# Longformer attention into a softplus layer: batch 2 at three slots a pair, other orders of loading, a second queue, and products that nobody reads

## The chip, the cores and the metric

The kernel runs on one core of a Trainium2 chip. The core has five engines that run side by side: TensorE (matrix products, into the accumulator memory PSUM), VectorE, ScalarE (activation functions such as Exp and Ln), GpSimd (POOL in the profile) and SyncE (SP), which here only issues DMA transfers. Each engine works through its own instructions in order, and semaphores hold an instruction until what it needs is there. The metric is the device time of one execution in microseconds (us), the median of several. TensorE's clock can be granted in full or at a lower share; the profile shows which.

## The reference

Eight batches of attention with 8 heads, 576 positions and 64 numbers per head. A query sees the keys within 32 positions and 8 global keys; the 8 global positions see everything. The result, 4608 tokens of 512 numbers, goes through a layer of 2048 softplus units and back to 512.

```python
scores = scale * np.matmul(q, k.transpose(0, 1, 3, 2))
mask = np.abs(pos[:, None] - pos[None, :]) <= window
mask = mask | is_global[:, None] | is_global[None, :]
scores = np.where(mask, scores, -1000000000.0)
attn = np.exp(scores - np.max(scores, axis=-1, keepdims=True))
attn = attn / (np.sum(attn, axis=-1, keepdims=True) + 1e-09)
x = np.matmul(attn, v)          # then (batch, position) x (head, number): 4608 x 512
h = x @ w_in                    # 4608 x 2048
g = np.maximum(h, 0.0) + np.log1p(np.exp(-np.abs(h)))
return g @ w_out                # 4608 x 512
```

## The kernel before

**Dense layers.** The 4608 tokens are nine tiles of 512. The main loop runs over tiles n = 0 to 9 and, in each, over 16 steps; a step is called a slot here, numbered 16 n + s. `mm1(n, s)` (L395) makes 128 of the 2048 units for tile n: four products of 128x512 into one of two PSUM buffers, then Exp (L403) and Ln (L404) on ScalarE. `mm2(n - 1, s)` (L408) makes a quarter of one 128-token block of the output of the tile before: four products; every fourth one is copied by VectorE (L418) and stored by SP (L419). So tile 0 has slots with first-layer products alone, tiles 1 to 8 have both, and the last 16 slots have second-layer products alone. The first weight comes in four chunks of 512 units (`load_w_in`, slots 4c to 4c + 3 of a tile need chunk c), the second in four chunks of rows (`load_w_out`); both are issued by GpSimd and converted to bf16 on the way.

**Attention** goes by batch and by pair of heads, four pairs a batch. Keys and queries come in rows of six positions (`load_runs`, one DMA a pair), are cast to bf16 (`cast_runs`) and transposed on TensorE (`transposes`, L253), with copies out of PSUM on VectorE (on ScalarE for the queries of batch 0). The columns of the 8 global positions are appended to each tile of 120 positions: for batches 0 and 1 by products with a one-hot matrix (L263), for the later ones from `glob_T`, which comes from DRAM through `gather`, `load_global_columns` and `global_columns` and is copied by GpSimd. `scores` are two groups of products, each followed by Exp; `mask` multiplies by a mask on VectorE; `sums` and `values` are passes of 12 products over the masked exponentials, with a matrix of ones and with V. `inv_ln` and `inv_exp` make 1 / sum as exp(-ln) on ScalarE; `scale_x` (L353) multiplies on VectorE into `xT`, which the dense layers read. `glob_sums`, `glob_norm` and `glob_out` do the same for the 8 global queries; `glob_out` (L369) is eight small GpSimd copies at positions held in registers. V is cast by GpSimd (`cast_v`, L120) with its global rows in the last 8 partitions of each tile (`load_v_rows`); batch 0 instead adds a second pass with the global rows `VG`, which `value_globals` makes by products.

**Buffers.** Scores, sums and values share one ring of PSUM regions, three in batch 0 and two afterwards; transposes have a ring of their own. The float rows of keys, queries and V have one buffer each, so the rows of a batch can be loaded only after those of the one before have been cast. `junk`, a slice of the second weight's tile, holds ones, and `warm` multiplies it by itself into a buffer that nobody reads.

**Order.** Everything is written out in order by hand. The prologue (L504 to L568) does batch 0, starts loads and casts of batch 1, then V's gather on GpSimd (behind `glob_out`), the gathers of keys and queries on SP, and `warm(4)`. In the main loop a plan says what is done after `mm1` (half 0) and after `mm2` (half 1) of each slot:

```python
for s in range(16):
    if n < n_tiles:
        mm1(n, s)
    attend(16 * n + s, 0)
    if n:
        mm2(n - 1, s)
    attend(16 * n + s, 1)
```

`at(g, half, ...)` puts a step there. From batch 4 on a pair takes four slots: transposes at half-slots 0 and 1 of the pair, scores at 4, sums and values at 8, the normaliser at 9, scaling at 10. Batches 1 to 3 (`START`) take two slots a pair from slots 3, 20 and 30, with the same numbers halved. `LOAD` and `CAST` say at which slots rows are loaded and cast; DMAs of SP and stores stand in one queue, and casts, gathers, weight loads and `glob_out` in GpSimd's one.

## Time and profile before

| | |
|---|---|
| median of 6 runs | 387.02 us (386.18 to 388.53) |
| the profiled execution | 385.48 us, its span 383.9 us |
| TensorE busy | 345.0 us (90%) |
| ScalarE busy | 275.2 us (72%) |
| VectorE busy | 183.3 us (48%) |
| GpSimd busy | 119.4 us (31%) |
| mean granted TensorE clock | 0.959 |

| stage | from to (us of the span) |
|---|---|
| prologue | 0 to 38.03 |
| tile 0, slots 0 to 15 | 38.03 to 75.19 |
| tiles 1 and 2, slots 16 to 47 | 75.19 to 163.30 |
| tiles 3 to 5, slots 48 to 95 | 163.30 to 273.70 |
| tile 6 to the end | 273.70 to 383.9 |

All times come from one profiled execution, from its first to its last instruction. PE is TensorE, PEld its loading of weights, DVE VectorE, ACT ScalarE, POOL GpSimd, SP the DMA queue of SyncE; L400 is line 400 of the kernel. Rows of the timeline give start, length, engine, line, operation, output and inputs, how many instructions are merged in the row and, in brackets, how long the engine was idle before and what ended that.

### The profile page before, as it was taken

How to read it: one execution, taken by the hardware profiler on the slowest of the kernel's cores; microseconds unless marked ns; L12 is line 12 of the kernel's file. 1: busy time of each engine (PE TensorE's matmuls, PEld its weight loads, DVE VectorE, ACT ScalarE, POOL GpSimd, SP SyncE). 2: the span in 40 equal slices, each digit the busy share in tenths (PEclk: the TensorE clock that was granted, in tenths of full speed). 3: DMA queues.
4: the chain of work that ended last, by engine and by line, in shares of the span. 5: the costliest groups of instructions: out<-in, count | busy, mean ns of one | idle time of the engine just before them, and what ended most of it. 6: DMA issues, size and time to landing. Idle time of an engine off the chain costs nothing.

```text
span 383.9 us, 7411 instructions
## 1 busy us (share of the span) xinstructions
PE 345.0 (90%) x2761; PEld 176.4 (46%) x2801; DVE 183.3 (48%) x485; ACT 275.2 (72%) x438; POOL 119.4 (31%) x275
## 2 busy tenths in 40 slices
PE   6587877798997889999999999999999999999984
PEld 3464443344544444555455545554554444444432
DVE  7664277415766664766567556656554200100111
ACT  5742698757876886888888888887888767776500
POOL 7961770446419304434081309311100100000000
PEclk9556899989999999999999999999999999999999
DMA  7999549979938605580669156700000010010111
GB/s 172 247 258 212 98 73 210 247 152 252 154 96 210 130 30 150 152 161 38 155 166 155 57 148 163 130 28 29 29 27 30 27 56 27 27 56 27 55 56 55
DMA packets 62495, 43.64 MB, mean 114 GB/s; under 512 B 40932, under 2 KB 57444, under 8 KB 62460
## 3 DMA queue, kind: packets, MB, share of 16 engines
q1 hardware_dynamic: 57836, 38.86, 42.2%
q0 software_dynamic: 4480, 4.31, 6.8%
q8 instruction: 22, 0.36, 0.4%
q14 instruction: 13, 0.11, 0.1%
q10 hardware_dynamic: 144, 0.01, 0.0%
HBM read 37.92 MB, written 9.81 MB: 124 GB/s over the span
## 4 chain that ended last, share of the span: by engine, by line
PE 56%; issue 11%; DMA 11%; POOL 7%; SPq 6%; DVE 4%; ACT 1%; another core or an unknown queue 1%; POOLq 1%; DVEq 0%
PE o L414 25%; PE hp L400 22%; PE av L325 4%; PE sc L291 2%; DMA q_f<-in_q_dram 2%; PE tp L258 2%; SPq L105 2%; SPq L96 2%; DMA v_f<-v_global_rows 2%; DMA v_f<-in_v_dram 2%; POOL V L122 2%; POOL qb L118 2%; DVE ex L304 2%; DMA q_global_rows<-in_q_dram 2%; DMA q_rows<-q_global_rows 1%
## 5 line engine op out<-in xcount | busy, mean ns | idle before, releaser
L400 PE MATMUL hp<-xT,w_in_t 128*128 128x512 bf16 x548 | 147.6, 386 | 3.8 <-POOL xT L372 2.3
L414 PE MATMUL o<-w_out_t,gt 128*128 128x512 bf16 x565 | 145.4, 381 | 4.4 <-DVE ot L418 3.3
L403 ACT ACTIVATE e<-hp 128x512 f32<-128x512 f32 x144 | 86.0, 597 | 60.6 <-PE hp L400 57.6
L404 ACT ACTIVATE gt<-e 128x512 bf16<-128x512 f32 x144 | 90.7, 630 | 4.5
L414 PEld LDWEIGHTS <-gt 128*128 128x128 bf16 x576 | 54.1, 98 | 67.7 <-issue 8.7
L400 PEld LDWEIGHTS <-w_in_t 128*128 128x128 bf16 x576 | 53.1, 99 | 65.9 <-issue 9.8
L418 DVE COPY ot<-o 128x512 f32<-128x512 f32 x36 | 24.8, 690 | 84.9 <-PE o L414 79.6
L304 DVE TENSOR_TENSOR ex<-ex,mask 128x1008 bf16<-128x1008 bf16 (+1 forms) x56 | 44.6, 805 | 28.7 <-ACT ex L299 27.8
L372 POOL COPY xT<-xg 128x4 bf16 x64 | 12.9, 201 | 126.9 <-DVE xg L367 123.5
L299 ACT ACTIVATE ex<-sc 128x1008 bf16<-128x1008 f32 (+1 forms) x56 | 48.5, 917 | 0.0
L122 POOL CAST V<-v_f 128x512 bf16<-128x512 f32 (+3 forms) x50 | 27.8, 595 | 39.4 <-DMA v_f<-v_global_rows 28.2
L344 ACT ACTIVATE rz<-av 128x616 f32<-128x616 f32 x32 | 21.7, 679 | 16.0 <-PE av L325 15.5
L291 PE MATMUL sc<-QT,KT 64*128 64x200 bf16 (+2 forms) x320 | 20.8, 250 | 12.9 <-DVE xT L359 6.4
L269 DVE COPY KT<-tp 128x480 bf16<-128x480 bf16 x32 | 20.9, 653 | 23.5 <-PE tp L258 15.0
L118 POOL CAST qb<-q_f 96x1024 bf16<-96x1024 f32 (+1 forms) x24 | 24.6, 1046 | 8.1 <-DMA q_f<-in_q_dram 8.1
L118 POOL CAST kb<-k_f 96x1024 bf16<-96x1024 f32 (+1 forms) x24 | 24.3, 1033 | 6.2 <-DMA k_f<-in_k_dram 3.4
L335 DVE TENSOR_REDUCE gs<-av 128x8 f32<-128x32 f32 x64 | 11.9, 187 | 28.8 <-ACT rz L344 23.8
L357 DVE TENSOR_TENSOR xT<-av,rz 128x480 bf16<-128x480 f32 x32 | 20.9, 655 | 9.3 <-ACT rz L348 9.1
L291 PEld LDWEIGHTS <-KT 64*128 64x128 bf16 x320 | 11.7, 97 | 27.0 <-issue 11.2
L269 DVE COPY QT<-tp 128x480 bf16<-128x480 bf16 x28 | 18.4, 657 | 10.9 <-PE tp L258 9.8
L348 ACT ACTIVATE rz<-rz 128x616 f32<-128x616 f32 x32 | 22.7, 710 | 0.4
L325 PE MATMUL av<-ex,ones 128*64 128x160 bf16 (+1 forms) x336 | 18.3, 233 | 4.3 <-DVE ex L304 3.9
...
## 6 DMA issues: line engine op xcount, KB each, us to landing
...
w_in_t<-in_moe_w_in_dram POOLq DMA_DIRECT2D x4, 512.0 KB, 13.9
w_out_t<-in_moe_w_out_dram POOLq DMA_DIRECT2D x4, 512.0 KB, 10.2
...
```

The source lines that it names most:

```text
L118: eng.tensor_copy(o, i)
L122: eng.tensor_copy(V1[b % 2][:rows, t, cols], v_f[:rows, t, cols])
L269: copy(dst[:, p, 0:4, 0:KW].rearrange("p t (q r) -> p t q r", r=RUN), spread[:, 0:4 * NQT].rearrange("p (t q) r -> p t q r", q=NQT))
L291: nc.tensor.matmul(out=sc[:, e, GOFF[t]:GOFF[t] + w], lhsT=KT[r, p, t, :], rhs=QT[r, p].rearrange("p t c -> p (t c)")[:, WLO[t]:WHI[t]], s ...
L299: nc.scalar.activation(out=ex, in_=sc[:, :, 0:GW[grp]], func=ACTF.Exp, scale=SCALE)
L304: nc.vector.tensor_tensor(out=ex, in0=ex, in1=masks[grp][:].unsqueeze(1).to_broadcast([P, 2, GW[grp]]), op=ALU.mult)
L325: nc.tensor.matmul(out=av[64 * e:64 * e + 64, OFF + lo:OFF + hi], lhsT=weight(t, e), rhs=exps[p, grp][rows, e, c:c + hi - lo], start=(j == ...
L400: nc.tensor.matmul(out=hp[:], lhsT=w_in_t[:, kd, kf * P:(kf + 1) * P], rhs=xT[:, kd, n * NT:(n + 1) * NT], start=(kd == 0), stop=(kd == KD ...
L403: nc.scalar.activation(out=e[:], in_=hp[:], func=ACTF.Exp)
L404: nc.scalar.activation(out=gts[n][:, kf, :], in_=e[:], func=ACTF.Ln, bias=1.0)
L414: nc.tensor.matmul(out=op[:], lhsT=gts[n][:, kf, i * P:(i + 1) * P], rhs=w_out_t[:, kf, :], start=(kf == 0), stop=(kf == KF - 1))
L418: nc.vector.tensor_copy(ot[:], op[:])
```

## The change

Slots and half-slots as above; "ahead of" and "behind" mean the order in which an engine gets its instructions.

- **Pace.** `PACE` gives each early batch its first half-slot, the half-slots per pair and the offsets of its steps. Batch 1 keeps two slots a pair and begins at slot 1.5 instead of 3; batch 2 takes three slots a pair from slot 16.5 (before: two from 20); batch 3 three and a half from slot 28.5 (two from 30); later batches keep four slots a pair and begin one slot later.
- **Loads of batches 0 to 2.** The queries of batch 0 go on ScalarE's queue, its keys and then V on SP's. Batch 2's keys and queries are loaded before the main loop, ahead of the gathers on SP, and cast from slot 11 instead of 16.
- **Weights.** Chunk 0 of the first weight is issued between casts of batch 0, chunk 1 behind `glob_out(0)`, chunks 2 and 3 and the second weight in slot 0 behind the V casts of batch 1 (before: all of the first weight in the prologue, the second in slot 5).
- **GpSimd's order.** V's gather and all eight casts of batch 1's keys and queries stand ahead of `glob_out(0)` (before: four casts, and the gather behind it).
- **Masks.** Made for two tiles at a time: group 0 in six instructions on GpSimd, group 1 in three on VectorE.
- **Batch 0.** Values of a pair are split in the pass with V and the one with the global rows; the first pair's V pass goes ahead of the scores of pair 2, the others behind the next scores. Exponentials of the first pair's second group come behind the next pair's transposes.
- **Unread products.** 14 of 512 columns ahead of transposes and six of 224 columns ahead of sums, all in batch 0, and `warm(14)` instead of `warm(4)`.
- **Global columns** are gathered for batches 2 to 7 only, loaded at slot 9 instead of before the loop, and transposed at slot 14 instead of 15.

```diff
+    FIRST = {"v": 1, "k": 2, "q": 2}
+    GB = B - FIRST["k"]
...
-    def load_runs(n, b, pairs=range(NP)):
+    grow = {n: nc.dram_tensor(f"{n}_global_rows", (NG, (B - FIRST[n]) * HD), FP32, kind="Internal").ap()
...
+    def load_runs(n, b, pairs=range(NP), eng=nc.sync):
         for p in pairs:
             hs = slice(2 * p, 2 * p + 2)
-            nc.sync.dma_start(out=runs[n][:, hs], in_=src[n][b, hs].rearrange("h (p r) d -> p h (r d)", r=RUN))
+            eng.dma_start(out=runs[n][:, hs], in_=src[n][b, hs].rearrange("h (p r) d -> p h (r d)", r=RUN))
...
+    def gather(n, eng):
+        first = FIRST[n]
         sv = src[n].rearrange("b h s d -> (b h) s d")[first * H:]
         for g in range(NG):
-            eng.dma_start(out=grow[n][g:g + 1, first * HD:].rearrange("o (c d) -> c o d", d=D),
+            eng.dma_start(out=grow[n][g:g + 1].rearrange("o (c d) -> c o d", d=D),
                           in_=sv[:, bass.ds(regs[eng][g], 1), :])
...
+    load_runs("q", 0, eng=nc.scalar)
     nc.scalar.preload_act_table_set("natural_log_exp_and_others")
-    for p in range(2):
-        load_runs("k", 0, [p])
-        load_runs("q", 0, [p])
+    load_runs("k", 0)
...
-    load_v(0, half_heads[0])
-    for p in range(2, NP):
-        for n in "kq":
-            load_runs(n, 0, [p])
-    load_v(0, half_heads[1])
+    for h in range(2):
+        load_v(0, half_heads[h])
...
-    masks = [const.tile([P, GW[i]], BF16, name=f"mask{i}") for i in range(2)]
...
-    def build_masks(tiles, eng):
-        for t in tiles:
...
+    masks = [const.tile([P, 200 * n], BF16, name=f"mask{i}") for i, n in enumerate((3, 2))]
...
+    def times(eng, o, cols, tiles, n):
+        eng.tensor_tensor(out=o, in0=band[:, cols].unsqueeze(1).to_broadcast([P, n, w]),
+                          in1=akey[:, tiles].unsqueeze(2).to_broadcast([P, n, w]), op=ALU.mult)
...
+    def build_mask_0(eng):
+        times(eng, m[:, :, 0:160], slice(40, 200), slice(0, 2), 2)
+        times(eng, masks[0][:, 160:560].rearrange("p (t c) -> p t c", c=200)[:, :, 0:40], slice(0, 40), slice(1, 5, 3), 2)
+        eng.tensor_scalar(out=m[:, :, 0:KW], in0=m[:, :, 0:KW], scalar1=ukey[:], scalar2=None, op0=ALU.add)
+        eng.tensor_scalar(out=masks[0][:, 400:496], in0=band[:, 40:136], scalar1=akey[:, 4:5], scalar2=ukey[:],
+                          op0=ALU.mult, op1=ALU.add)
+        valid(eng, m[:, :, KW:P], slice(0, 2), 2)
+        valid(eng, masks[0][:, 496:504].unsqueeze(1), slice(4, 5), 1)
...
+    def build_mask_1(eng):
+        times(eng, m, slice(0, 200), slice(2, 4), 2)
+        eng.tensor_scalar(out=m[:, :, 40:160], in0=m[:, :, 40:160], scalar1=ukey[:], scalar2=None, op0=ALU.add)
+        valid(eng, m[:, :, 160:168], slice(2, 4), 2)
...
-    def transposes(n, b, p, copy=nc.vector.tensor_copy):
...
+        for _ in range(unread):
+            nc.tensor.matmul(out=ps[:], lhsT=junk[:, 0:P], rhs=junk[:], start=True, stop=True)
         for r in range(RUN):
             nc.tensor.transpose(out=tb[:, r * NQ:(r + 1) * NQ], in_=rows[:, r, p * P:(p + 1) * P],
                                 identity=ident_bf[:NQ, :NQ])
...
+    SC = {}
+
+    def products(b, p, grp):
+        sc = SC[p, grp] = region(b, "sc")[:].rearrange("p (e c) -> p e c", e=2)
...
+    def scores(b, p, grp):
+        products(b, p, grp)
+        exponentials(b, p, grp)
...
+    def over_keys(b, p, z, weight, rows=slice(0, P), first=True, last=True, unread=0):
+        if first:
+            AV[p, z] = region(b, "av")
+        av = AV[p, z]
+        for _ in range(unread):
+            nc.tensor.matmul(out=av[:, 0:OFF], lhsT=junk[:, 0:P], rhs=junk[:, 0:OFF], start=True, stop=True,
+                             skip_group_check=True)
...
+    def sums(b, p, unread=0):
+        over_keys(b, p, 1, lambda t, e: ones[:], unread=unread)
...
+        over_keys(b, p, 0, lambda t, e: V1[b % 2][:, t, p * P + 64 * e:p * P + 64 * e + 64], last=b > 0)
+
+    def values_of_globals(b, p):
+        over_keys(b, p, 0, lambda t, e: VG[96:P, p * P + 64 * e:p * P + 64 * e + 64], rows=slice(96, P), first=False)
...
-            grows[n] = work.tile([B * NG, HD], FP32, tag=f"ex{0 if n == 'k' else 1}", bufs=2, name=f"{n}_rows")
-            nc.sync.dma_start(out=grows[n][:], in_=grow[n].rearrange("g (b c) -> (g b) c", b=B))
+            grows[n] = work.tile([GB * NG, HD], FP32, tag=f"ex{0 if n == 'k' else 1}", bufs=2, name=f"{n}_rows")
+            nc.sync.dma_start(out=grows[n][:], in_=grow[n].rearrange("g (b c) -> (g b) c", b=GB))
...
-    LOAD = {2: (5, 6, 7), 3: (20, 20, 20), 4: (30, 30, 31)}
-    CAST = {2: 16, 3: 26}
-    START = {1: 3, 2: 20, 3: 30}
-    for p in range(2, NP):
-        for m in "kq":
-            at(p, 0, cast_runs, m, 1, pair_heads(p), slice(0, RUN), nc.gpsimd)
+    LOAD = {2: (None, None, 5), 3: (17, 18, 19)}
+    CAST = {2: 11, 3: 23}
+
+    PACE = {1: (3, 4, 2, 4, 5, 5), 2: (33, 6, 3, 6, 7, 8), 3: (57, 7, 4, 7, 8, 9)}
     for h in range(2):
         for t in range(NTL):
-            at(4, 0, cast_v, 1, t, nc.gpsimd, half_cols[h])
+            at(0, 0, cast_v, 1, t, nc.gpsimd, half_cols[h])
+    for c in range(2, 4):
+        at(0, 0, load_w_in, c)
     for c in range(4):
-        at(5, 0, load_w_out, c)
+        at(0, 0, load_w_out, c)
+    at(9, 0, load_global_columns)
     for n in "kq":
-        at(15, 1, lambda n: global_columns(n), n)
+        at(14, 1, global_columns, n)
...
-            at(loads[0], 1, load_runs, "k", b)
-            at(loads[1], 1, load_runs, "q", b)
+            if b > 2:
+                at(loads[0], 1, load_runs, "k", b)
+                at(loads[1], 1, load_runs, "q", b)
...
+        start, pair, to_scores, to_sums, to_inverse, to_x = PACE.get(b, (2 * g0 - 11, 8, 4, 8, 9, 10))
         for p in range(NP):
-            r = 4 * p - 7
-            step(r, 1, transposes, "k", b, p)
-            step(r + 1, 0, transposes, "q", b, p)
-            step(r + 2, 1, scores, b, p, 0)
-            step(r + 2, 1, scores, b, p, 1)
...
-            step(r + 4, 1, sums, b, p)
...
-            step(r + 5, 0, glob_sums, b, p, 0)
-            step(r + 5, 0, inv_exp, p)
-            step(r + 5, 1, scale_x, b, p)
...
+            h = start + pair * p
+            step(h, transposes, "k", b, p)
+            step(h + 1, transposes, "q", b, p)
+            step(h + to_scores, scores, b, p, 0)
...
+            step(h + to_sums, sums, b, p)
+            step(h + to_sums, values, b, p)
+            step(h + to_sums, inv_ln, b, p)
+            step(h + to_inverse, inv_exp, p)
+            step(h + to_x, scale_x, b, p)
+        step(h + to_x + 1, glob_norm, b)
+        step(h + to_x + 1, glob_out, b)
+        for h in sorted(steps):
+            for f, a in sorted(steps[h], key=lambda fa: fa[0] is not transposes):
+                at(h // 2, h % 2, f, *a)
...
-    build_masks([4], nc.gpsimd)
-    build_masks([3], nc.scalar)
-    build_masks([2], nc.gpsimd)
+    build_mask_0(nc.gpsimd)
     warm(11)
...
-    build_masks([0, 1], nc.vector)
-    for t in range(NTL):
-        cast_v(0, t, nc.gpsimd, half_cols[0])
+    build_mask_1(nc.vector)
     for p in range(2, NP):
         for n in "kq":
             cast_runs(n, 0, pair_heads(p), ALL, nc.gpsimd)
-    load_w_in(0)
-    for t in range(NTL):
-        cast_v(0, t, nc.gpsimd, half_cols[1])
-    for c in range(1, 4):
-        load_w_in(c)
+        for t in range(NTL):
+            cast_v(0, t, nc.gpsimd, half_cols[p - 2])
+        if p == 2:
+            load_w_in(0)
     load_positions(nc.gpsimd, mybir.EngineType.Pool)
-    scores(0, 0, 0)
-    scores(0, 0, 1)
+    for grp in range(2):
+        products(0, 0, grp)
+    exponentials(0, 0, 0)
     for p in range(NP + 1):
         if 0 < p < NP:
             mask(p, 0)
         if p + 1 < NP:
-            transposes("k", 0, p + 1)
+            transposes("k", 0, p + 1, unread=3 if p < 2 else 2)
+        if p == 0:
+            transposes("q", 0, 1, act_copy, unread=2)
+            exponentials(0, 0, 1)
+            mask(0, 0)
         if p < NP:
-            if not p:
-                mask(p, 0)
             mask(p, 1)
         if p:
-            sums(0, p - 1)
+            sums(0, p - 1, unread=3 if p < 3 else 0)
             inv_ln(0, p - 1)
-        if p + 1 < NP:
-            transposes("q", 0, p + 1, act_copy)
+        if p and p + 1 < NP:
+            transposes("q", 0, p + 1, act_copy, unread=2)
         if p:
             inv_exp(p - 1)
+        if p in (1, 3):
+            value_globals(half_cols[p // 2])
+        if p == 1:
+            values(0, 0)
         if p + 1 < NP:
             scores(0, p + 1, 0)
             scores(0, p + 1, 1)
+        if p > 1:
+            values(0, p - 1)
         if p:
-            if p in (1, 3):
-                value_globals(half_cols[p // 2])
-            values(0, p - 1)
+            values_of_globals(0, p - 1)
             glob_sums(0, p - 1, 0)
             scale_x(0, p - 1)
         if p == 2:
             for i in range(NP):
                 for m in "kq":
                     load_runs(m, 1, [i])
-    for i in range(2):
+    gather("v", nc.gpsimd)
+    for i in range(NP):
         for m in "kq":
-            cast_runs(m, 1, pair_heads(i), slice(0, RUN), nc.gpsimd)
+            cast_runs(m, 1, pair_heads(i), ALL, nc.gpsimd)
+    load_v(1)
+    load_v_rows(1)
     glob_norm(0)
     glob_out(0)
-    load_v(1)
-    gather("v", nc.gpsimd, 1)
-    load_v_rows(1)
+    load_w_in(1)
     load_positions(nc.sync, mybir.EngineType.SP)
     for n in "kq":
+        load_runs(n, 2)
+    for n in "kq":
         gather(n, nc.sync)
-    load_global_columns()
-    warm(4)
+    warm(14)
 
     start_psum.__exit__(None, None, None)
```

## The prediction

> **What bounds the kernel now.** I read the page's span and engine rows first, then the same rows cut at the stage borders of the program: the first product of the dense layers (38.03 us), token tile 1 (75.19), tile 3 (163.30) and tile 6 (273.70). The columns are busy time of each engine with its instruction count, granted TensorE clock, DMA share, GB/s.
>
> ```profile
> span 383.9 us, 7411 instructions
> 11.40:35.30 23.90, 19.68 (x234) 14.19 (x236) 14.45 (x43) 12.32 (x22) 14.05 (x18) 0.50 1.16 243
> 38.03:75.19 37.16, 27.84 (x299) 14.89 (x304) 19.91 (x65) 30.69 (x48) 17.81 (x36) 0.95 0.81 154
> 75.19:163.30 88.11, 79.56 (x686) 40.57 (x696) 49.20 (x125) 66.06 (x101) 39.13 (x86) 0.98 0.63 149
> 163.30:273.70 110.40, 108.64 (x925) 55.81 (x936) 67.23 (x162) 92.80 (x145) 36.19 (x92) 1.00 0.47 107
> ```
>
> Tiles 3 to 5 are full: TensorE idles 1.76 us in 110.40, and a tile with one batch of attention takes 36.80. Tiles 1 and 2 carry the same work, plus about one pair, in 88.11 instead of 73.6, and TensorE idles 8.55. Tile 0 is ScalarE's (30.69 of 37.16). Ahead of it, most of the prologue runs at half clock.
>
> Second, the timeline of ScalarE, for the cost of a pair of heads in tiles 1 and 2 (two slots a pair) and in the full tiles (four):
>
> ```profile
> 103.78 0.60 ACT L403 ACTIVATE e<-hp 128x512 f32<-128x512 f32 x1 [0.38 <-PE hp L400]
> 110.28 0.60 ACT L403 ACTIVATE e<-hp 128x512 f32<-128x512 f32 x1 [0.37 <-PE hp L400]
> ...
> 174.68 0.60 ACT L403 ACTIVATE e<-hp 128x512 f32<-128x512 f32 x1
> 183.71 0.60 ACT L403 ACTIVATE e<-hp 128x512 f32<-128x512 f32 x1
> ```
>
> Two slots with a pair take 6.50; four take 9.03. A slot without attention takes 1.73 (81.41 to 83.13 in the same view), so four slots at the old spacing cost 6.50 + 2 x 1.73 = 9.96, which is 0.93 a pair more. TensorE's timeline has most of that: the second group of scores waits for a PSUM region that VectorE's scaling frees:
>
> ```profile
> 108.07 0.35 PE L291 MATMUL sc<-QT,KT 64*128 64x200 bf16 x4 [0.71 <-DVE xT L359]
> ```
>
> Third, GpSimd's timeline, for what ends the prologue and what the weights queue behind:
>
> ```profile
> 24.18 0.82 POOL L118 CAST kb<-k_f 96x768 bf16<-96x768 f32 x1
> 24.95 1.16 POOL L118 CAST qb<-q_f 96x768 bf16<-96x768 f32 x1
> 35.90 2.09 POOL L372 COPY xT<-xg 128x4 bf16 x8 [9.79 <-DVE xg L367]
> 38.45 4.56 POOL L105 DMA_DIRECT2D v_global_rows<-in_v_dram  x8 [0.46 <-issue]
> ...
> 48.06 4.28 POOL L122 CAST V<-v_f 128x256 bf16<-128x256 f32 x10 [1.93 <-DMA v_f<-v_global_rows]
> ```
>
> The first dense product waits for the eight copies at 35.90, and these for the TensorE chain of batch 0. GpSimd is idle for the 9.79 us before.
>
> **The change part by part.** The sum is against the profiled execution: 385.48 us for a span of 383.9, 1.5 under the median of 387.02.
>
> *Middle (slots 16 to 47).* Batch 2 goes to three slots a pair, batch 3 to three and a half, every later batch starts one slot later. No work goes; 8 pairs lose up to 0.93 each, 7.4. Two other measures stand beside it: idle time over that of full tiles, 8.55 - 1.76 x 88.11/110.40 = 7.1, and length over that of full tiles, 88.11 - 73.6 - 2.1 for one pair more (9.03 - 4 x 1.73) - 1.7 for 3.4 at half clock from 76.3 = 10.7. Slot 32 alone took 4.75 where its like took 3.25, its masks 2.46 instead of 1.30 beside GpSimd casts; such casts stay, so I add half of that 1.5. Against it: in batch 2 the normaliser's second exponential now stands behind a dense slot's two activations on ScalarE (0.60 + 0.63), which delays the scaling and so the next scores. Between values and next scores stand three blocks of four products and a transpose (3 x 0.865 + 0.42 = 3.0, plus 0.4 of first scores); the chain is 2.15 to the start of that exponential, 0.72, then 0.90 of scaling, 3.8. So 0.4 a pair stays on batch 2, 1.6. Gain 7.4 + 0.7 - 1.6 = 6.5; ends 3.9 (7.1 less 0.4 on all eight pairs) and 9.1 (10.7 less the 1.6). The queries' and keys' GpSimd copies stay ahead of the casts in their slots. Later batches have full tiles, and one slot later still ends 4 slots ahead of the tile that needs them: nothing; were that cover gone, a slot is 1.73.
>
> *Prologue, bounded by GpSimd.* GpSimd is free at 26.11 now. It gains four casts of batch 1 ahead of the eight copies (4 x 0.83 = 3.3) and the eight V gathers (4.56), and loses three weight issues (2.23): free at 31.8. Its rows must be there: by the page's GB/s 6.49 MB have moved at 28.8; batch 0 (3.54), batch 1's k and q (2.36) and one weight chunk (0.52) are 6.42, and two last casts follow, 30.2. Mask building swaps seven instructions of 0.30 to 0.86 (4.1) for six wider ones for which no row exists: between 2 and 6 in all, taken equal, since 0.86 for 120 columns is the nearest row. Copies at 31.8, first dense product at 34.0 instead of 38.03: 4.0 less.
>
> *Prologue, TensorE's chain*, which must be done by 31.8 and ends at 35.8 now. One pass of 12 products takes 0.96 at half clock and 0.58 at full (timeline rows at 27.56 and 104 us); 11 passes and two global-value products follow 19.17, so full clock is worth 11 x 0.38 + 2 x 0.6 = 5.4. VectorE builds masks in three operations (about 1.25, by the 0.66 of a 480-column product) instead of seven (2.4), ScalarE in none instead of four (1.3). Added: 14 unread products of 512 columns and six of 224, 14 x 0.216 + 6 x 0.1 = 3.6 at full clock, 7.2 at half. TensorE idles 4.2 of the 23.9, chiefly ahead of the transposes and scores where the unread ones stand, which hides about 3. The values no longer stand ahead of the scores for the global rows' product. End about 30 to 32, so GpSimd decides. Without the full clock it ends at 36 to 37.
>
> The clock row: granted 0.50 from 11.4 to 35.3 with TensorE busy 19.7 of 23.9. The Trainium skill's TensorE: Matmul & The Clock Gate (section HAM oscillation) has the gate close after idle gaps over some 3.4 us. By that alone the clock would have stayed full here and the unread products would buy nothing: the prologue's gain would be VectorE's 1.2 less whatever of the 3.6 is uncovered, an estimate of about zero. The row differs: no such gap exists and the clock is half, so narrow products seem not to count as full ones, and I go by the row.
>
> *Warm-up before the dense layers.* 14 products instead of 4: 3.0 at full clock, within the wait for the copies; at half clock 14 x 0.43 = 6.0, which would end some 2 late. Taken hidden. With the clock up, slots 0 to 2 (1.71, 1.50, 1.16 between their first activations) go to about 1.2 each: 0.7 less.
>
> *Second queue.* ScalarE issues four query loads (4 x 0.45 = 1.8) ahead of its table load; its first cast waits till 5.20 anyhow (2.58 idle); without that cover it costs the 1.8. DMA moved 172 GB/s in the first 9.6 us and 247 in the next, so up to (0.247 - 0.172) x 9.6 = 0.7 MB or 3 us could come sooner; taken as 0, as GpSimd bounds the end. V's first half now lands behind all rows of batch 0, about 14 instead of 11; its casts end near 15 and the product that reads them stood at 17.99.
>
> In DMA: Bandwidth & Descriptors (Issuing engines are not separate DMA queues) the Trainium skill speaks against this part: a second queue saves issue time alone. By it the sum has at most the 1.8 of SP's issue time here; I have 0.
>
> *Weights later.* Chunk 1 of the first weight is issued after the copies, at 34.0 to 34.8, and slot 4 needs it about 7.9 later (first activations of slots 0 to 3 at 1.2, 1.2, 2.8, 2.7). The trace gives 11.8 to 17.9 from issue to landing for this weight in crowded traffic, 5.8 to 14.3 for the other:
>
> ```profile
> DMA to landing us min/median/max: 11.8/13.9/17.9
> ...
> DMA to landing us min/median/max: 5.8/10.2/14.3
> ```
>
> Stall = 0.8 + landing - 7.9: none at 5.8, 3.1 at 10.2, 4.7 at 11.8. One chunk beside batch 2's eight row loads lies between 5.8 and 11.8: 9, a stall of 2.0. Chunks 2 and 3 and the second weight stand behind the ten V casts (4.28), which wait for batch 1's V and its global rows. These are gathered some 14 us earlier than at 38.45 and V's 1.18 MB follow by about 34, so the casts run 37 to 41.3, values of pair 0 get their half in time and chunk 2 is issued at 42, needed at slot 8, about 54: covered; without that cover each us late is a us.
>
> *Global columns* move a slot earlier, and read six batches rather than eight (48 rows, not 64). The stall that they make (ScalarE idle 2.13 at 76.33, then a window at half clock) keeps its cause, an activation buffer that comes free late: nothing.
>
> **Sum:** -6.5 - 4.0 - 0.7 + 2.0 = -9.2, 385.5 to 376.3, and with the median's 1.5, 377.8.
>
> **Rivals.** *The prologue keeps half clock:* TensorE ends at 36 to 37 with a warm-up of 6.0 behind it, dense products start 1 to 3 later than before; 377.8 + 4.0 + 2 = 384. For it: 2.0 us of narrow products in one window were not enough to hold the clock at 11.4. Against: 1.08 us of wide ones now stand in that stretch.
>
> *No stall on the weights, and rows sooner by the second queue:* 377.8 - 2.0 - 2 = 373.8. For it: the 172 GB/s; against: 11.8 for the same chunk under the same kind of traffic.
>
> *Slower: V of batch 1 stays late.* If its global rows land at T, chunk 2 lands at T + 4.3 + 0.9 + 5.8 and is due at 54, so T over 43 stalls, T at today's 48 costs 5, and the two later chunks 3 to 4 each beside the second weight's queue; with T past 49 the 9.2 is eaten: 387 to 391. For it: GpSimd is one queue in order; against: DMA has 5 us in hand by bytes.
>
> **How the numbers follow.** Chances: forecast 0.48, half clock 0.18, no stall 0.21, late V 0.13. Ends: 385.5 - 9.1 - 6 (masks 2 cheaper) - 0.7 + 0 + 1.5 = 371.2, rounded down for the second queue, and 384 to 386 from the half-clock case. Within 0.3% (386 to 388), about what this kernel's measurement can tell from no change, I put 0.04, from both high cases; above it 0.12.
>
> **What would show it.** Right: granted clock near 1.0 between 11 and 35 us; eight copies starting near 32 with GpSimd busy before them; two-slot spacing of 6.5 gone, pairs of batch 2 about 7.7 apart, tiles 1 and 2 together near 81.5; a wait of the fifth slot's products for the weight of about 2. Wrong: TensorE waiting for the weight at slots 4, 8 or 12 in many us, the copies released by VectorE at 35 again, or scores in batch 2 waiting 0.7 for the scaling.

## The result and the profile after

| | before | after |
|---|---|---|
| median | 387.18 us (385.12 to 389.19, 71 runs) | 390.91 us (385.13 to 394.84, 34 runs) |
| the profiled execution, its span | 385.48, 383.9 | 386.6, 385.0 |
| mean granted TensorE clock | 0.959 | 0.973 |

The ratio of after to before is 1.0042, 95% interval 1.0025 to 1.0060: slower by 0.4%, or by 1.0% of the medians, where 2.4% less was forecast. A ratio here leaves out every execution more than 1.5% above the fastest of its kernel (about half of those of after, none of before), so it can differ from the quotient of two medians, which is 1.0096 for after.

The profiled execution of after is one of its quick ones, 4.3 under the median, so it does not show all of the loss. Its span and its stages, in the columns of the table of before (busy time of each engine with its instructions, granted clock, DMA share, GB/s); the first row is the prologue from 9.50 on, the next tile 0, then tiles 1 and 2, and tiles 3 to 5:

```profile
span 385.0 us, 7462 instructions
9.50:33.10 23.60, 19.26 (x283) 12.86 (x283) 16.93 (x49) 14.65 (x28) 19.82 (x32) 0.86 1.14 237
35.48:77.20 41.72, 28.09 (x297) 16.21 (x302) 20.99 (x66) 29.79 (x46) 12.96 (x28) 0.88 0.99 188
77.20:160.70 83.50, 78.22 (x675) 39.98 (x685) 44.67 (x120) 65.22 (x101) 37.36 (x84) 0.98 0.56 138
160.70:273.00 112.30, 109.95 (x925) 55.68 (x936) 60.91 (x163) 93.58 (x145) 38.50 (x93) 1.00 0.47 105
```

The prologue's clock rose from 0.50 to 0.86, tiles 1 and 2 are shorter, tile 0 is longer with nearly the same busy time of TensorE (28.09 against 27.84), and tiles 3 to 5, forecast unchanged, are longer too. For comparisons I measure every stage from the start of a slot's first activation (`e<-hp`, L403 before, L422 after) to that of the next stage's first slot; the last column ends with the span. `all_three` is the best version found by the experiments.

| us | prologue | tile 0 | tile 1 | tile 2 | tiles 3 to 5 | tile 6 to end | span |
|---|---|---|---|---|---|---|---|
| before | 39.31 | 37.02 | 44.11 | 43.97 | 110.43 | 109.05 | 383.9 |
| after | 36.54 | 43.40 | 43.24 | 38.58 | 112.34 | 110.88 | 385.0 |
| difference | -2.8 | +6.4 | -0.9 | -5.4 | +1.9 | +1.8 | +1.1 |
| all_three | 34.62 | 39.40 | 43.89 | 38.58 | 112.34 | 110.88 | 379.7 |

Batch 2's pairs, in ScalarE's timeline of after (start, length): three slots take 7.98, from 92.69 to 100.67, where two took 6.50.

```profile
92.69 0.60 ACT L422 ACTIVATE e<-hp 128x512 f32<-128x512 f32 x1
95.69 0.60 ACT L422 ACTIVATE e<-hp 128x512 f32<-128x512 f32 x1
98.69 0.60 ACT L422 ACTIVATE e<-hp 128x512 f32<-128x512 f32 x1 [0.67 <-PE hp L419]
100.67 0.60 ACT L422 ACTIVATE e<-hp 128x512 f32<-128x512 f32 x1
```

GpSimd's timeline at the end of the prologue: casts right up to the copies, which start at 33.08, and the weight chunk behind them. TensorE's: slot 4 waits for that chunk.

```profile
32.15 0.82 POOL L122 CAST qb<-q_f 96x768 bf16<-96x768 f32 x1
33.08 2.04 POOL L391 COPY xT<-xg 128x4 bf16 x8
35.25 0.77 POOL L443 DMA_DIRECT2D w_in_t<-in_moe_w_in_dram  x1
```

```profile
45.03 1.04 PE L419 MATMUL hp<-xT,w_in_t 128*128 128x512 bf16 x4 [1.03 <-DMA w_in_t<-in_moe_w_in_dram]
```

Where the new time in tile 0 is spent is read from the chain of waits through slots 4 to 6 of after (start, length, what; "issue" is time that nothing in the profile explains):

```profile
45.03 1.05 PE hp L419 x4
46.10 0.60 ACT e L422
46.73 0.63 ACT gt L423
47.36 0.61 ACT rz L364
48.00 0.66 DVE xT L376
48.66 0.18 DVE xT L378
48.88 0.51 PE sc L299 x4
...
53.48 1.21 PE hp L419 x4
54.71 0.60 ACT e L422
...
57.49 0.52 PE sc L299 x4
```

The second exponential of the normaliser (`rz` L364) stands behind the dense slot's two activations, the scaling behind it, the second group of scores behind the scaling, and the next dense products behind those. One pair takes 8.61 (48.88 to 57.49), the next 7.80, both partly at half clock (47.1 to 53.9, 57.3 to 60.7); how much of that is the order and how much the clock is read from a run at full clock further down.

### The profile page after: what moved, and what is told of

Same layout as the page of the kernel before. It is cut to its first block, busy times and chain, and to the rows that moved or that the text cites. A ratio compares the mean times of both kernels' runs of the same rounds, so it can differ in the third digit from the quotient of the medians.

```text
span 385.0 us, 7462 instructions
## 1 busy us (share of the span) xinstructions
PE 347.8 (90%) x2790; PEld 176.0 (46%) x2831; DVE 174.3 (45%) x481; ACT 274.6 (71%) x434; POOL 118.6 (31%) x274
## 3 DMA queue, kind: packets, MB, share of 16 engines
q0 software_dynamic: 4480, 4.31, 6.7%
## 4 chain that ended last, share of the span: by engine, by line
PE 66%; DVE 9%; issue 7%; DMA 6%; POOL 5%; ACT 5%; SPq 0%; POOLq 0%; ACTq 0%
PE o L433 28%; PE hp L419 26%; PE av L341 6%; DVE ot L437 3%; PE tp L264 3%; PE sc L299 3%; DMA w_in_t<-in_moe_w_in_dram 3%; DVE QT L275 2%; DMA v_f<-in_v_dram 2%; DMA k_f<-in_k_dram 2%; ACT e L422 1%; ACT gt L423 1%; POOL qb L122 1%; POOL V L126 1%; POOL xT L391 1%
## 5 line engine op out<-in xcount | busy, mean ns | idle before, releaser
L422 ACT ACTIVATE e<-hp 128x512 f32<-128x512 f32 x144 | 86.0, 597 | 59.0 <-PE hp L419 55.6
L391 POOL COPY xT<-xg 128x4 bf16 x64 | 16.5, 258 | 138.6 <-DVE xg L386 135.0
L319 DVE TENSOR_TENSOR ex<-ex,mask 128x1008 bf16<-128x1008 bf16 (+1 forms) x56 | 37.3, 671 | 46.3 <-ACT ex L310 45.1
L299 PE MATMUL sc<-QT,KT 64*128 64x200 bf16 (+2 forms) x320 | 19.7, 245 | 11.0 <-DVE xT L378 4.4
L122 POOL CAST kb<-k_f 96x1024 bf16<-96x1024 f32 (+1 forms) x24 | 23.5, 1006 | 2.8 <-DMA k_f<-in_k_dram 2.7
L122 POOL CAST qb<-q_f 96x1024 bf16<-96x1024 f32 (+1 forms) x24 | 23.2, 993 | 1.2 <-PE tp L264 1.1
L364 ACT ACTIVATE rz<-rz 128x616 f32<-128x616 f32 x32 | 22.6, 705 | 0.1
L299 PEld LDWEIGHTS <-KT 64*128 64x128 bf16 x320 | 10.9, 95 | 23.0 <-issue 11.7
```

What stands on the lines that cost most here:

```text
L122: eng.tensor_copy(o, i)
L299: nc.tensor.matmul(out=sc[:, e, GOFF[t]:GOFF[t] + w], lhsT=KT[r, p, t, :], rhs=QT[r, p].rearrange("p t c -> p (t c)")[:, WLO[t]:WHI[t]], s ...
L319: nc.vector.tensor_tensor(out=ex, in0=ex, in1=masks[grp][:, 0:GW[grp]].unsqueeze(1).to_broadcast([P, 2, GW[grp]]), op=ALU.mult)
L422: nc.scalar.activation(out=e[:], in_=hp[:], func=ACTF.Exp)
```

## The experiments

Unless said otherwise each edit is to the changed kernel. A time is a median with its range; the stages are those of the table above.

### One suspect at a time

**Odd start.** Batch 1 begins at half-slot 3; before, its steps began at 6 and had the same spacing. Tile 0 has no second-layer products, so nothing stands between half 0 and half 1 of a slot, while `mm1` stands between half 1 and the next half 0. With an odd start the queries' transposes (half 0) and the scores that need them (half 1) come back to back, and between the sums (half 1) and the second exponential (half 0) comes a dense slot.

```diff
-    PACE = {1: (3, 4, 2, 4, 5, 5), ...}
+    PACE = {1: (4, 4, 2, 4, 5, 5), ...}
```

> The changed kernel with batch 1 begun half a slot later (first half-slot 4 instead of 3), nothing else. Theory A (the odd half-slot is what lengthened tile 0: tile 0 has no second-layer products, so scores now stand directly behind the query transposes and wait 1.0 for the copies, and the normaliser's second exponential stands behind a dense slot's activations): a pair returns from 8.6 to about 5.9, tile 0 from 43.4 to 36 to 38, the whole 6 to 7 less, about 384 by the median. Rival B (late weights and row traffic): tile 0 keeps 42 to 43, the whole moves by less than 1. Rival C (the clock falls by itself in tile 0, whatever the order): half-clock windows between 47 and 61 stay and tile 0 loses 2 to 3 only.

Measured 388.40 (386.73 to 389.76), ratio 1.0015 (0.9984 to 1.0046). Tile 0 fell from 43.40 to 37.24, its pairs 5.87 apart and all at full clock (1.00 from 42 to 78 us); but the prologue of the profiled execution took 45.24. A large part of the cause stands in VectorE's and GpSimd's timelines of that run:

```profile
29.44 6.13 DVE L319 TENSOR_TENSOR first_ex<-first_ex,mask 128x1008 bf16<-128x1008 bf16 x2
35.49 0.18 DVE L351 TENSOR_REDUCE gs<-av 128x8 f32<-128x32 f32 x1
```

```profile
27.82 0.52 POOL L109 DMA_DIRECT2D v_global_rows<-in_v_dram  x1 [2.17 <-DMA w_in_t<-in_moe_w_in_dram]
28.34 0.84 POOL L122 CAST kb<-k_f 96x768 bf16<-96x768 f32 x1
...
33.73 0.82 POOL L122 CAST qb<-q_f 96x768 bf16<-96x768 f32 x1
41.59 2.04 POOL L391 COPY xT<-xg 128x4 bf16 x8 [7.04 <-DVE xg L386]
```

Two masks, 1.16 together in the next run, took 6.13: they ended 1.0 after the last of the eight casts (34.55), and what follows of the last pair, the copies included, waited for them. This hold is 5.0 of the 9.3 us by which the prologue is longer than that of the run with four casts below. Another 3.5 had been lost before: these masks started at 29.44 against 25.90 there, about half of it because an earlier mask stood 2.55 beside other casts at 16.64. Behind the hold the clock was 0.50 from 36 to 40. The series itself started late, because the last gather of V stood 2.17 before it, which the profile puts down to the landing of the weight chunk ahead of it on GpSimd's queue.

**Weight chunk 1 earlier**, right behind chunk 0.

```diff
         if p == 2:
             load_w_in(0)
+            load_w_in(1)
...
     glob_out(0)
-    load_w_in(1)
```

> The changed kernel with chunk 1 of the first weight issued right behind chunk 0 in the prologue instead of behind the eight copies, nothing else. Theory A: only the wait of 1.0 for the weight at slot 4 goes, so tile 0 loses about 1, less what the prologue's rows lose to the chunk (0.5 MB, up to 2 later): -1 to +1 in all. Rival B (late weights and traffic are what lengthened tile 0): 3 to 6 less.

Measured 392.20 (391.08 to 393.55), ratio 1.0140 (1.0094 to 1.0186): worse. The gather now waited 4.31 for the weights, the eight casts moved to 32.16 to 38.4, and this time the last product before the copies was the one held, until the last cast had ended; it takes 0.19 elsewhere. On VectorE's timeline:

```profile
33.89 4.52 DVE L386 TENSOR_TENSOR xg<-gs 128x32 bf16<-128x32 f32 x1
```

The scaling (0.66) and the reciprocal (0.34) directly ahead of it, which do not read two inputs from SBUF (the on-chip memory beside PSUM), took their usual time beside the same casts.

**Later batches back** to their old slots.

```diff
-    ... PACE.get(b, (2 * g0 - 11, 8, 4, 8, 9, 10))
+    ... PACE.get(b, (2 * g0 - 13, 8, 4, 8, 9, 10))
```

> The changed kernel with batches 4 to 7 begun one slot earlier, at the slots of the kernel before, nothing else. Theory D (one slot later puts every output copy behind the first reduction on VectorE in the same half-slot, and the next second-layer products wait for the copy, since their PSUM buffer is single): slots 48 to 95 go from 37.45 a tile to 36.8 to 36.9, the rest behind them by 1.5 to 2 less, the whole 3 to 4 less. Rival E (batch 3 at three and a half slots runs into batch 4 and pushes work into tiles 3 on, or the traffic did it): tiles 3 to 5 stay at 37.4 and the whole moves by less than 1.

Measured 390.61 (386.98 to 394.06), ratio 1.0083 (1.0035 to 1.0132). Tiles 3 to 5 took 109.87 instead of 112.34 and the rest 109.62 instead of 110.88: 3.7 less. But tile 2 went from 38.58 to 42.54, its slots 43 and 44 from 2.47 and 2.89 to 4.71 and 4.17, where batch 3's last pair now meets batch 4's first. So what the later slot costs behind tile 2 it saves in tile 2. What the later slot costs is read from tile 3 of after. On VectorE the copies of the queries and the sums of the global positions now fall into the slot of the output copy `ot` and stand ahead of it, and the next `o` products, which have one buffer, wait for that copy: they begin 1.11 after the dense block ahead of them, where 0.86 is usual. VectorE's timeline, then TensorE's:

```profile
169.32 0.66 DVE L275 COPY QT<-tp 128x480 bf16<-128x480 bf16 x1 [0.51 <-PE tp L264]
...
170.36 0.69 DVE L437 COPY ot<-o 128x512 f32<-128x512 f32 x1
```

```profile
169.12 1.03 PE L433 MATMUL o<-w_out_t,gt 128*128 128x512 bf16 x4
169.99 1.03 PE L419 MATMUL hp<-xT,w_in_t 128*128 128x512 bf16 x4
171.10 1.02 PE L433 MATMUL o<-w_out_t,gt 128*128 128x512 bf16 x4
```

**Even start and later batches back** together.

> Both of these edits of the plan together: batch 1 at half-slot 4, later batches one slot earlier. If theories A and D are both right and stand in different stages, the gains add: 9 to 11 less than the changed kernel, about 376 to 378 in the profiled execution, faster than both kernels. If one of them only moves the loss, the sum falls short by that much.

Measured 388.16 (385.22 to 389.42), ratio 1.0005 (0.9975 to 1.0035). The later tiles and tile 2 were as in the run before this one; tile 0 took 42.68 although its start was even, 3.46 of it a wait of slot 4 for the weight. So freeing one thing let the next show.

**Four casts in a series**, the other four behind batch 0's outputs and weight chunk 1, as the kernel before had it.

```diff
-    for i in range(NP):
+    for i in range(2):
         for m in "kq":
             cast_runs(m, 1, pair_heads(i), ALL, nc.gpsimd)
...
     glob_out(0)
     load_w_in(1)
+    for i in range(2, NP):
+        for m in "kq":
+            cast_runs(m, 1, pair_heads(i), ALL, nc.gpsimd)
```

> The changed kernel with the casts of batch 1's last two pairs (four of the eight GpSimd casts) moved from ahead of the eight copies to behind them and behind the second weight chunk. Theory F (GpSimd casts back to back keep VectorE's instructions with two SBUF inputs, the masks and the last product of the global queries, from starting: 6.13 for two masks in the run with the even start, 4.52 for the last product in the one with the early weight; how much is hit depends on where the casts fall, so the time from run to run spreads): first activation of the dense layers at 33.5 to 36 in the profile, no VectorE instruction of the prologue over 2.5, and the times of all runs within 2% instead of 385 to 395, median 2 to 4 under the changed kernel. Rival G (the spread comes from the landing of rows, not from the casts): first activation still anywhere between 36 and 45 and the same spread. Rival H: the later casts push V's casts, and pair 0's values wait in tile 0 by 2 to 3, so nothing is gained.

Measured 386.87 (384.44 to 391.79), ratio 0.9988 (0.9956 to 1.0021). The last pair's masks went back to 0.67 and 0.56 and the prologue took 35.94. But the step from slot 14 to 15 grew from 4.09 to 7.82, in waiting for the global columns.

**Eight casts in the kernel before**, ahead of its `glob_out(0)`.

```diff
-    for p in range(2, NP):
-        for m in "kq":
-            at(p, 0, cast_runs, m, 1, pair_heads(p), slice(0, RUN), nc.gpsimd)
...
-    for i in range(2):
+    for i in range(NP):
         for m in "kq":
             cast_runs(m, 1, pair_heads(i), slice(0, RUN), nc.gpsimd)
```

> The kernel before with one part of the change: all eight casts of batch 1's keys and queries ahead of the eight copies, instead of four there and four in slots 2 and 3. Theory F: the four more casts at about 26 to 30 meet the masks of the fourth pair at 28.7 to 29.9, which then take 2 to 4 instead of 1.16, and the prologue, whose products are the longer chain at half clock, ends 1 to 3 later, with more spread; tile 0 loses at most 1. Rival G: GpSimd is idle there for 9.79, so nothing moves: same within 0.3%.

Measured 387.01 (385.28 to 392.02), ratio 0.9970 (0.9928 to 1.0012): no harm. There the last four casts each waited 0.32 to 1.20 for their rows, so the series has gaps; the two masks beside it took 1.78. The long holds all stand in series without gaps. But such a series does not always hold to its end: in after itself the second of two masks came in behind the first cast, and it was the next cast that took longer. VectorE's timeline, then GpSimd's:

```profile
25.88 1.78 DVE L319 TENSOR_TENSOR first_ex<-first_ex,mask 128x1008 bf16<-128x1008 bf16 x2
```

```profile
26.34 0.90 POOL L122 CAST kb<-k_f 96x768 bf16<-96x768 f32 x1
27.18 1.17 POOL L122 CAST qb<-q_f 96x768 bf16<-96x768 f32 x1
```

What decides between the two is not shown; it would make the prologue differ from one execution to the next.

**Odd start in the kernel before.**

```diff
-                    at(START[b] + (r + 7) // 2, (r + 7) % 2, f, *a)
+                    h = (r + 7) + (b == 1)
+                    at(START[b] + h // 2, h % 2, f, *a)
```

> The kernel before with one change: batch 1's steps all one half-slot later, so that they start at an odd half-slot as in the changed kernel. Theory: tile 0 then takes 42 to 44 us instead of 37.0 (pairs 8.6 apart instead of 5.87), and the global columns follow without a wait: time 390 to 394. Rival, that the odd start costs only with the changed kernel's other orders (columns late, weight late): tile 0 stays within 1.5 of 37.0, time 386 to 389.

Measured 388.30 (386.66 to 390.09), ratio 1.0006 (0.9980 to 1.0032). Tile 0 took 41.46 instead of 37.02, tile 1 42.80 instead of 44.11. The stage shows the theory's cost, nearly; the time shows the rival's. The two profiled executions stand 1.7 below and 1.8 above their medians, so the profiles exaggerate, and some of the loss is found again in tile 1.

### The gate behind the others

**Several at once:** even start, four casts, later batches back, and batch 3 at three slots a pair.

```diff
-    PACE = {1: (3, 4, 2, 4, 5, 5), 2: (33, 6, 3, 6, 7, 8), 3: (57, 7, 4, 7, 8, 9)}
+    PACE = {1: (4, 4, 2, 4, 5, 5), 2: (33, 6, 3, 6, 7, 8), 3: (57, 6, 3, 6, 7, 8)}
...
```

> The changed kernel with four edits: batch 1 at half-slot 4, four casts moved as in the run above, batches 4 to 7 one slot earlier and batch 3 at three slots a pair (offsets of batch 2), so that it is out of the way of batch 4. If theories A, D and F hold and the 4.0 that slots 32 to 47 took back in the run with the earlier batches was the meeting of batches 3 and 4: first activation 33.5 to 36, tile 0 at 36.5 to 39 (the upper end with the weight's wait of up to 3.5), tile 2 at 39 to 40, tiles 3 to 5 at 36.62, the whole 374 to 379 in the profile, faster than both kernels. If the meeting of batches 3 and 4 has another cause, tile 2 stays at 42.5 and the whole at 377 to 382.

Measured 388.70 (387.29 to 391.69), ratio 1.0059 (1.0026 to 1.0092). The prologue took 35.06, the pairs in tile 0 were 5.86 apart, and slot 14 was reached at 66.1; then one step of 12.45. Slot 15 began at 78.5; in the run with four casts it had been 78.2. Whatever came sooner, this moment stayed, so something arrives at a fixed time. Tile 2 was 42.81 here, although batch 3 now keeps out of batch 4's way: the meeting of the two is not what makes it long when the later batches start a slot earlier, and the cause of that stays open.

**Even start and four casts alone**, to be rid of the other edits.

> Even start and four casts, with the global columns' loads still behind batch 2's V. It prices the order on SyncE's queue: the k_rows loads are issued at 68 to 70, the step at slot 14 is 9 to 12 us as in the combined run (12.45), and the time 386 to 388, 6 above the run with all three. If that step was of the combined run's other edits (later batches back, batch 3 at three slots): 381 to 383.

Measured 388.67 (386.43 to 390.92), ratio 1.0043 (1.0015 to 1.0070); the step at slot 14 is 11.65. VectorE's and SP's timelines of this run name what it waits for:

```profile
74.18 0.86 DVE L403 CAST k_rows_bf<-k_rows 48x512 bf16<-48x512 f32 x1 [9.21 <-DMA k_rows<-k_global_rows]
```

```profile
52.55 5.87 SPq L109 DMA_DIRECT2D q_global_rows<-in_q_dram  x8
58.53 10.11 SPq L99 DMA_DIRECT2D v_f<-in_v_dram  x5
68.69 0.42 SPq L103 DMA_DIRECT2D v_f<-v_global_rows  x1
69.21 0.33 SPq L399 DMA_DIRECT2D k_rows<-k_global_rows  x1
```

The loads of the global columns are planned at slot 9, batch 2's V at slot 5, both on SP's queue. SP issues each as soon as its turn comes, and V's five transfers take 10.11 to issue. Before the change the columns were loaded ahead of the loop and went out at 57.74.

**Columns first:** V of batch 2 planned at slot 9, behind them.

```diff
-    LOAD = {2: (None, None, 5), 3: (17, 18, 19)}
+    LOAD = {2: (None, None, 9), 3: (17, 18, 19)}
```

> The changed kernel with one number changed: batch 2's V is loaded at slot 9 instead of slot 5, so that the loads of the global columns stand ahead of it on SyncE's queue. Theory: in the run with four casts and in the combined run the first dense products stood still at slot 14 (steps of 7.82 and 12.45 us instead of about 3) because the loads of k_rows were issued at 68.7 and 69.5, behind 10 us of V loads; now they should be issued at about 57.5, as before the change. Alone this frees little, because with batch 1's odd start tile 0 comes to slot 14 only at 74.2: the step 4.09 falls to 3.4 at most, time 385.5 to 388. Rival, that the loads are late because of the gathers in front of them: issue stays near 67 and nothing changes.

Measured 391.73 (383.94 to 394.11), ratio 0.9968 (0.9913 to 1.0023). In the profiled execution (391.97) the prologue took 44.87, with masks held 5.97 beside the eight casts, and tile 0 came to slot 14 only at 79.41, so the columns were not what it waited for there: the step stayed at 3.97. They were issued at 66.74, about when the rival had said, but not because of the gathers: SP waited 10.4 for a mask and 1.9 for the sums and values that read it, since these rows take a buffer of the exponentials.

**All three:** even start, four casts, columns first.

> Three gates opened together: batch 1 starts on an even half-slot, only four casts stand in one series ahead of batch 0's global outputs, and the loads of the global columns go ahead of batch 2's V. Theory: each of the three alone gave nothing because the next one took its place. Together: first exponential at 35 to 36.5, tile 0 in 35.5 to 37.5 (pairs 5.87 apart, step at slot 14 of about 3), tiles 1 and 2 in 81.5, the rest as in the changed kernel: span 376 to 378.5, time 378 to 381, ratio about 0.98. Rival, that slot 14 waits for something else that is there only at 76 to 78 (the gathers themselves, batch 2's rows): the step at slot 14 stays above 8 and the time at 385 to 389.

Measured 380.65 (379.24 to 385.74, six executions), ratio 0.9810 (0.9760 to 0.9861): 1.9% faster than the kernel before. SP's timeline, with the columns at 58.04 instead of 69.21:

```profile
52.08 5.85 SPq L109 DMA_DIRECT2D q_global_rows<-in_q_dram  x8
58.04 0.51 SPq L399 DMA_DIRECT2D k_rows<-k_global_rows  x1
62.85 0.32 SPq L399 DMA_DIRECT2D q_rows<-q_global_rows  x1
63.22 6.83 SPq L99 DMA_DIRECT2D v_f<-in_v_dram  x5
```

The step at slot 14 is 4.84 and slot 15 begins at 72.4. Slots 3 and 4 take 4.15 and 3.63 instead of 2.77 and 3.10: the weight.

**Leaving out one of the three** each time: the casts (`even_cols`), and the even start (`four_cols`); the columns were left out above.

> The same without the change to the casts: all eight stand in one series on GpSimd. Theory: the end of the prologue then depends on where the masks and the last product of VectorE fall in that series, 36.5 to 45 from one execution to the next; median 381 to 386, with a wider spread than with four casts. If the series is harmless on the whole: within 1 us of the run with all three.

> The changed kernel with four casts in a series and the global columns' loads ahead of batch 2's V, but batch 1 still at its odd half-slot. Beside the run with all three (380.65) it prices the odd start alone. If the odd start is the large cost that tile 0 showed (8.6 us a pair instead of 5.87), tile 0 is 42 to 43 and the time 383 to 385. If it costs little, as the run of the kernel before with an odd start (388.3 against 387.2) suggests, because what tile 0 loses is found again in the first steps of tile 1: 381 to 382.

Measured: without four casts 388.26 (383.03 to 390.38), ratio 0.9974 (0.9932 to 1.0015); without the even start 385.02 (380.57 to 392.22), ratio 0.9915 (0.9882 to 0.9948). With those above there is a run of every combination of the three; ratios to the kernel before:

| | eight casts, columns late | eight, columns first | four, columns late | four, columns first |
|---|---|---|---|---|
| odd start | 1.0042 (after) | 0.9968 | 0.9988 | 0.9915 |
| even start | 1.0015 | 0.9974 | 1.0043 | 0.9810 |

Against the corner 0.9810, undoing one costs 4.1 us (start), 6.3 (casts) and 9.0 (columns; each a difference of ratios times 387.2, good to about 2.5 by the two intervals). The start brings 4.1 in the last column and no gain in the others (in the third the even start is 2.1 slower, at the edge of what the intervals show). None of the three can be priced alone: each hides the others.

The run without the even start also parts the order from the clock. Its tile 0 is at full clock until 62 us, and its pairs are 6.49 apart there, against 5.87 with an even start; TensorE's timeline:

```profile
49.64 0.35 PE L299 MATMUL sc<-QT,KT 64*128 64x200 bf16 x4 [1.02 <-DVE xT L378]
...
56.13 0.34 PE L299 MATMUL sc<-QT,KT 64*128 64x200 bf16 x4 [1.02 <-DVE xT L378]
```

So the order itself takes 0.6 a pair, and the rest of the 8.61 and 7.80 in after came with the half clock.

### What was left of the forecast

**Weight chunk 1 ahead of the four casts**, on top of all three.

```diff
     gather("v", nc.gpsimd)
+    load_w_in(1)
     for i in range(2):
```

> All three, and weight chunk 1 issued on GpSimd ahead of the four casts instead of behind batch 0's global outputs. Theory: the wait of about 1.9 us for that chunk in slots 3 and 4 (steps 4.15 and 3.63 against 2.77 and 3.10) goes: tile 0 37.5, time 378 to 380. Rival: the chunk, 0.76 us of issue earlier on the queue, pushes the casts back and takes DMA time from batch 1's V and the gathers; the first exponential comes later by as much: 380 to 382.

Measured 380.80 (378.95 to 385.66), ratio 0.9824 (0.9794 to 0.9855): no gain. The wait at slot 4 went and tile 0 fell to 36.22, but the prologue took 36.56 instead of 34.62 and tile 1 44.73 instead of 43.89. The time is the rival's. Its mechanism is not shown: the casts did start 3.5 later (29.31), but the copies waited for VectorE's last product (33.15), and that chain was late from a mask held 2.48 at 17.38, ahead of the chunk.

**Without the unread products**, on top of all three (`unread=0` everywhere, `warm(4)`), and without them in the changed kernel itself.

> The kernel with all three gates open (380.65), without the unread products and with the old warm-up of four. It prices them where nothing later hides the prologue. My forecast had 5.4 us of TensorE time for the full clock against 3.6 of added products, TensorE's chain ending at 30 to 32 with them and at 36 to 37 without: time 384 to 386, first exponential at 38.5 to 40, clock half through the prologue. If the clock rises anyhow, or the chain is not what ends the prologue: 380 to 382.

> The changed kernel without any of the unread products ahead of transposes and sums, and with the warm-up of 4 products again. The prediction's account (they keep the clock at full, worth 5.4, for 3.6 of work): half clock from about 10 to 35, the prologue's TensorE chain 3 to 6 longer, first activation 1 to 5 later than with them. Rival (they do not set the clock, or the chain is not what ends the prologue): first activation within 1 of the changed kernel's, whatever the clock.

Measured 385.27 (383.44 to 388.33), ratio 0.9963 (0.9930 to 0.9996), against 0.9810 with them; the prologue 39.18 against 34.62, of which 1.6 is a mask that met the four casts (2.26 against 0.67). In the changed kernel: 391.32 (387.48 to 394.38), ratio 1.0076 (1.0040 to 1.0113) against 1.0042, where the eight casts can hide the rest. One stretch of the prologue, without and with them, both on top of all three, in the columns of the stage table:

```profile
10.00:33.00 23.00, 19.06 (x244) 14.37 (x244) 15.19 (x40) 13.48 (x27) 15.89 (x27) 0.50 1.12 237
```

```profile
10.00:33.00 23.00, 19.35 (x285) 12.52 (x287) 15.70 (x48) 14.18 (x28) 18.91 (x36) 0.93 1.10 228
```

TensorE is busy for nearly the same time in both, 19.06 and 19.35; the clock is 0.50 and 0.93.

**Batch 0's queries back on SP's queue**, on top of all three.

```diff
-    load_runs("q", 0, eng=nc.scalar)
...
+    for p in range(2):
+        load_runs("k", 0, [p])
+        load_runs("q", 0, [p])
```

> The kernel with all three gates open, with batch 0's queries back on SyncE's queue in the old order (two pairs of K and Q, half of V, two pairs, the other half). My forecast took the second queue at 0, with 3 us as the most it could bring. If it carries part of the prologue's gain: first exponential 1.5 to 3 us later, time 382 to 384. If not: 380 to 381.5.

Measured 382.13 (379.38 to 384.48), ratio 0.9863 (0.9794 to 0.9932); the interval overlaps that of all three, so whether the second queue brings anything, 1.5 us by the medians, stays open.

**The pace alone, in the kernel before:** batches 2 and 3 at the new half-slots, with their casts and batch 3's loads moved to match; prologue, loads of batch 2, queues and columns as before.

```diff
-    LOAD = {2: (5, 6, 7), 3: (20, 20, 20), 4: (30, 30, 31)}
-    CAST = {2: 16, 3: 26}
-    START = {1: 3, 2: 20, 3: 30}
+    LOAD = {2: (5, 6, 7), 3: (17, 18, 19)}
+    CAST = {2: 11, 3: 23}
+    START = {1: 3}
+    PACE = {2: (33, 6, 3, 6, 7, 8), 3: (57, 7, 4, 7, 8, 9)}
...
```

> The kernel before with only batch 2's and batch 3's pairs at the changed kernel's half-slots (and batch 2's casts at slot 11, batch 3's loads and casts as in the changed kernel); prologue, queues, even start of batch 1 and columns in their old places. Theory: tiles 1 and 2 together 81.5 to 83 instead of 88.1, the rest as before: time 380.5 to 382.5. Rival, that the pace needs the earlier rows of batch 2: its K and Q are issued only at 64, land at about 70 and are cast by 77, and its first transposes at slot 16 wait: tile 1 grows by 2 to 5 and the time is 382.5 to 387.

Measured 391.76 (390.17 to 392.26), ratio 1.0112 (1.0083 to 1.0141). GpSimd's timeline:

```profile
73.71 3.19 POOL L118 CAST kb<-k_f 96x1024 bf16<-96x1024 f32 x3 [18.99 <-DMA k_f<-in_k_dram]
79.20 1.04 POOL L118 CAST qb<-q_f 96x1024 bf16<-96x1024 f32 x1 [2.29 <-DMA q_f<-in_q_dram]
80.19 2.03 POOL L372 COPY xT<-xg 128x4 bf16 x8
```

Batch 2's first casts stood 18.99 waiting for rows, and behind them, in the same queue, batch 1's eight copies, which the first products of tile 1 need; those waited 6.9, tile 0's last step was 11.52 and tile 0 45.14. The rival named the late rows, but not that they would hold batch 1. Tile 2 was 42.54 here too; the later batches had their old slots here as in the run with the later batches back. So the pace and the early rows belong together.

## Why the prediction was wrong, and where it was right

*Middle, -6.5 (ends 3.9 and 9.1).* Measured 81.82 for tiles 1 and 2 instead of 88.08, 6.3 less; 81.5 had been named. Three slots took 7.98, not 7.7, and the scores waited 0.50 for the scaling instead of 0.71. This step was right, also in size.

*Later batches one slot later, nothing.* Wrong: +3.7 in the profile, about 0.25 a pair from an output copy that now stands behind other instructions of VectorE. The step looked only at whether the batches were in time, not at the half-slot in which each of their instructions falls. With the 6.3 it belongs to, the middle's net gain is 2.5.

*Prologue, -4.0, GpSimd the bound at 31.8, TensorE's chain ending at 30 to 32.* The clock (0.86 from 9.50 to 33.10) and the bound were right: the copies follow the last cast at 33.08 in after, and with four casts the prologue is 4.7 shorter than before (34.62 against 39.31), VectorE's last product ending the chain at 30.4. The unread products are worth 4.6 us by the medians, 5.9 by the ratios, which fits the forecast of TensorE ending at 36 to 37 without them. The row that was weighed against the Trainium skill's TensorE: Matmul & The Clock Gate (section HAM oscillation) was the one to go by: with TensorE nearly equally busy and no gap over 1.7 us from 10 to 33 us in either run, the clock was 0.50 or 0.93, as wide products were missing or there.

The step that failed here is "four casts of batch 1 ahead of the eight copies (4 x 0.83 = 3.3)". They were costed as time on GpSimd alone. In a series without gaps they can also hold VectorE's masks and last product, on which the same copies wait; in the two profiled executions with prologues of 44.9 and 45.2 that took 4.8 and 5.0. Four casts in place of eight are worth 6.3 us where nothing else hides it.

*Tile 0: warm-up -0.7, weight +2.0 (0 to 4.7).* The weight was right: 1.03 in after, 1.8 with all three, 3.46 and 0 in others. That its removal brings nothing was not foreseen. What failed is a step that isn't there: batch 1's new start was described, "keeps two slots a pair and begins at slot 1.5", and given no cost. It made the stage 6.4 longer in the profile, 1.0 of it the weight's wait. Of the rest some 2.5 is the order itself (0.6 for each of four pairs, an estimate from the spacing at full clock), and the remainder came with the half clock; whether the odd start brought that on is not shown. By the times the start is worth 4.1 once the other gates are open.

*Global columns, nothing: "keeps its cause, an activation buffer that comes free late".* Wrong at the decisive place. Their loads were moved from ahead of the loop to slot 9, and the step did not follow them past the V loads of batch 2 on SP, planned at slot 5. That delays them by 11 us (58.04 against 69.21), and in no profiled execution with this order did slot 15 begin before 78.2, where the kernel before had 72.95. In the profiled execution of after it began at 78.3 with tile 0 slow, so the loss was covered and the trace of after doesn't name it: there VectorE's cast last waited for ScalarE. With the other two gates open it costs 9.0 us by the ratios, 6.8 of it in the step itself (11.65 against 4.84).

*Second queue, 0.* Not refuted, not shown.

*The sum.* Forecast 376.3 for the execution of 385.48, a change of -9.2. After's own profiled execution is +1.1: the prologue gave 1.2 less than forecast, tile 0 is 5.1 too long, the later batches 3.7, the middle 0.2 (differences of the stage table). With all three repaired it was 381.29 (span 379.7): prologue -4.7, tile 0 +2.4, tiles 1 and 2 -5.6, the rest +3.7, together -4.2. The forecast lacks the 3.7 of the later batches and has tile 0 too short by 1.1 and the middle by 0.9; the prologue gave 0.7 more than forecast.

*The signs.* Nearly all that the prediction named as signs of being right came in after: the clock at 0.86, the copies at 33.08, tiles 1 and 2 in 81.82, a wait of 1.03 for the weight. They stood at the parts that had been given a cost; the loss stood at those that had been put at nothing.

*The rivals.* None of the three happened as written. The one on half clock counts 2.0 us of narrow products ahead of 11.4; the trace has 1.46 us of TensorE busy from 8.0 to 11.4. The slower one, batch 1's V late, looked for the block in GpSimd's queue; V was in time (its casts ran from 37.82 in after), and it was SP's queue that blocked.

What is left open: why four casts leave all three's own times between 379.24 and 385.74, and how the 390.91 of after divides between executions. If everything after the first activation took as long as in the profiled one (348.4), the median would mean a prologue of about 40.9; this is an estimate and no run shows it. A part of the spread may be earlier holds: in the profiles without the even start and with the early chunk on top of all three, a mask of batch 0 stood 1.80 and 2.48 at about 18, beside casts of batch 0's last pair and V, where all three had 0.62, and the last pair's masks began at 27.98 and 27.47 instead of 24.57.
